# Local-and-global attention with an ELU feed-forward: scales of w_in from sums on ACT, three groups of weight pairs, zero matmuls between attention's steps

## The chip, the cores and the metric

The kernel runs on one core of one Trainium2 chip. The metric is the device time in microseconds of the execution, as the median of several runs. PE is the matrix engine (TensorE; PEld its weight loads), DVE the vector engine, ACT the scalar engine, POOL GpSimd, and SP the engine whose queue issues the transfers.

## The reference

Eight batches of eight heads with 512 local and 32 global positions of 64 elements. A local query sees the 32 global keys and the local keys at most 32 positions away; a global query sees everything. The 4608 rows of the result (512 wide) go through a feed-forward network.

```python
k_all = np.concatenate([k_g, k_l], axis=2);  v_all = np.concatenate([v_g, v_l], axis=2)
out_g = np.matmul(sm(scale * np.matmul(q_g, k_all.transpose(0, 1, 3, 2))), v_all)
s_ll = np.where(np.abs(pos[:, None] - pos[None, :]) <= 32, scale * (q_l @ k_l^T), -1e9)
a_l = sm(np.concatenate([scale * (q_l @ k_g^T), s_ll], axis=-1))
out_l = np.matmul(a_l, v_all)
x = concatenate([out_g, out_l], axis=2) as rows of 512
h = x @ w_in                                        # 512 x 2048
g = np.where(h > 0.0, h, np.exp(np.minimum(h, 0.0)) - 1.0)
return g @ w_out                                    # 2048 x 512
```

(The lines are shortened; `sm` is the softmax over the last axis.)

## The kernel before

**Attention** is a generator over slots. Each batch has ten: two for the global queries and eight local ones (two groups of four heads, four tiles of 128 queries). A slot has four steps, between which control is handed back: S (scores, `stage_s`, matmuls at L458; for a global slot `stage_ga`, L406), T and U (transposes of the probabilities, L494, two slots later) and V (values, `stage_v`, L516, three slots later). The index `i` of the main loop counts these steps. DVE adds the mask to the scores and takes the maximum (L469), ACT makes the exponentials (L476), POOL divides (L483).

**The feed-forward network** runs in fp16 with three products for each one (high x high, low x high, high x low). Its x is cut in 17 blocks of 256 rows, sixteen local ones and one with all the global rows; `split_x` makes the high and low parts of a block when attention has completed it. The 2048 inner columns are eight pairs of 2 x 128. For a block and a pair, `ffn1` makes the first half (24 matmuls, L231) and the elementwise step (ACT L239 and L240, POOL L241, DVE L246, ACT L248, DVE L249), and `ffn2`, two pairs later, the second half (12 matmuls, L273). Each half is cut in quanta, eight to a pair.

**The weights** arrive as 64-bit numbers and are converted on the chip, in 16 units: `unit(0, p)` for w_in, `unit(1, p)` for w_out. A unit is one load of 1 MB into one of two `raw` buffers, and then the steps `s0` to `s4`: ACT and POOL take the size of the value and clamp it (L151, L152), DVE puts the fp32 bits together in three passes (L156, L159, L163), the scale comes from a maximum (DVE, L168) for w_in and from a sum (ACT, L170) for w_out, ACT writes the high part (L181) and DVE the low one (L184). For w_in the scale is shared by all partitions: `all_max` transposes the column with a matmul (L106) and takes the maximum of it (L107).

**Groups.** A block's eight pairs can be done as one group ("f"), or, as long as not all weights are converted, in groups a, b, c, d of 1, 1, 2 and 4 pairs; `tables(group)` makes the factors of a group once its weights are there. Each group but the last of a block writes its partial output to `od` in DRAM; the next one reads it back and adds it on DVE (L281). `choose` takes the lowest ready block with a group that has its tables. Four blocks go through the groups; 13 go as "f".

**The order.** The main loop hands out steps of attention and quanta of the network by `PACE`, pairs of (step, quanta done by then), with straight lines between. Until the second entry's step `lead[0]` holds: attention runs alone. Units are started at listed steps, and later by a credit: 2 for each step of attention from 8 steps before the end of the lead, 1 for each quantum, and a unit for every `CONV` of it. `defer(n, fn)` runs a step n ticks later. The framework's scheduler then orders the instructions of each engine by their place in the program and by when it believes their inputs to be there, and inserts the semaphores. PSUM has two `h` buffers (values of attention in the lead, later the first halves), two `acc`, and four `pa`. Ten matmuls of zeros (`warm`, L117) stand at the start.

Of the kernel before, what the change touches and what calls it, by code (L numbers as in the profile page):

```python
# [10 lines left out]
F32 = mybir.dt.float32  # L11
F32R = mybir.dt.float32r
I32 = mybir.dt.int32
AF = mybir.ActivationFunctionType
ALU = mybir.AluOpType
# [6 lines left out]
DM, DF = 512, 2048  # L22
# [10 lines left out]
AHEAD = 2  # L33


PACE = ((0, 0), (66, 0), (112, 180), (320, 850))
WARM = 10
CONV = 14
NBL = B * SL // BLK
GROUPS = {"a": (0, 1), "b": (1, 2), "c": (2, 4), "d": (4, 8), "f": (0, 8)}  # L40
NX = 5


# [6 lines left out]
def attn_ffn(ctx: ExitStack, tc: tile.TileContext, qT, qgT, kT, vT, w_in, w_out, mask, out):  # L50
# [62 lines left out]
    wout = [wts.tile([P, NFT, DM], F16, name=f"wout{k}") for k in "hl"]  # L113
    warm = wout[0][:, NFT - 1, :]
    nc.vector.memset(warm, 0.0)
    for _ in range(WARM):
        nc.tensor.matmul(ps_o.tile([P, DM], F32, name="acc"), warm[:, 0:P], warm, start=True, stop=True)  # L117
    pww = wts.tile([P, NP], F32, name="pww")
    pwo = wts.tile([P, NP], F32, name="pwo")
    isc = wts.tile([P, NP], F32, name="isc")  # L120
# [13 lines left out]
    def unit(m, p):  # L134
        f = slice(2 * p * P, 2 * (p + 1) * P)
        shape = [P, NC, 2 * P] if m == 0 else [P, 2, DM]
        raw = ffn.tile([*shape, 2], I32, name="raw")
        if m == 0:
            nc.sync.dma_start(raw, w1[:, :, f, :])
            parts = [w[:, :, f] for w in win]  # L140
        else:
            nc.sync.dma_start(raw, w2[:, 2 * p:2 * p + 2, :, :])
            parts = [w[:, 2 * p:2 * p + 2, :] for w in wout]
        pw = (pww if m == 0 else pwo)[:, p:p + 1]
        u = ffn.tile(shape, F32, name="cu", bufs=3)
        mx = ffn.tile([P, 4], F32, name="cm", bufs=4)
        high, low = raw[..., 1], raw[..., 0]
        ui = u.bitcast(I32)

        def s0():  # L150
            nc.scalar.activation(u, high.bitcast(F32), AF.Abs)  # L151
            nc.gpsimd.tensor_scalar(u, u, FMAX, FMIN, ALU.min, ALU.max)  # L152

        def s1a():
            tc.keep_in_program_order(
                nc.vector.tensor_scalar(ui, ui, 3, 0x3ffffff8, ALU.logical_shift_left, ALU.bitwise_and))  # L156

        def s1b():
            nc.vector.scalar_tensor_tensor(out=ui, in0=high, scalar=-0x40000000, in1=ui,  # L159
                                           op0=ALU.bitwise_and, op1=ALU.bitwise_or)  # L160

        def s1c():
            nc.vector.scalar_tensor_tensor(out=ui, in0=low, scalar=29, in1=ui,  # L163
                                           op0=ALU.logical_shift_right, op1=ALU.bitwise_or)

        def s1d():
            if m == 0:
                nc.vector.tensor_reduce(out=mx[:, 0:1], in_=u, op=ALU.max, axis=AX.XY, apply_absolute_value=True)  # L168
            else:
                nc.scalar.activation(low.bitcast(F32), u, AF.Abs, accum_out=mx[:, 1:2])  # L170

        def s2():
            if m == 0:
                all_max(mx[:, 1:2], mx[:, 0:1])

        def s3():
            nc.vector.tensor_scalar_max(mx[:, 1:2], mx[:, 1:2], LOW)
            power(pw, mx[:, 1:2])
            nc.vector.reciprocal(mx[:, 2:3], pw)
            nc.vector.tensor_scalar_mul(mx[:, 3:4], mx[:, 2:3], 2.0 ** 14)  # L180
            nc.scalar.activation(parts[0], u, AF.Copy, scale=mx[:, 3:4])  # L181

        def s4():
            nc.vector.scalar_tensor_tensor(out=parts[1].rearrange("p a b -> p (a b)") if m else parts[1],  # L184
                                           in0=u.rearrange("p a b -> p (a b)") if m else u, scalar=mx[:, 3:4],
                                           in1=parts[0].rearrange("p a b -> p (a b)") if m else parts[0],
                                           op0=ALU.mult, op1=ALU.subtract)

        d = 1 if lead[0] else 2
        lag = 7 if m else 12  # L190
        for i, fn in ((1, s0), (1 + d, s1a), (1 + 2 * d, s1b), (1 + 3 * d, s1c), (1 + 4 * d, s1d),
                      (1 + lag, s2), (2 + lag, s3), (3 + lag, s4)):
            defer(i, fn)

    def tables(group):

        r = slice(*GROUPS[group])
        wm = wts.tile([P, 4], F32, name=f"wm_{group}")
        t = wts.tile([P, NP], F32, name=f"t_{group}")
        kk = wts.tile([P, NP], F32, name=f"kk_{group}")  # L200
        nc.vector.tensor_mul(t[:, r], pww[:, r], pwo[:, r])
        nc.vector.tensor_reduce(out=wm[:, 0:1], in_=t[:, r], op=ALU.max, axis=AX.X)

        def rest():
            all_max(wm[:, 1:2], wm[:, 0:1])
            nc.vector.reciprocal(wm[:, 2:3], wm[:, 1:2])
            nc.vector.tensor_scalar(t[:, r], pwo[:, r], wm[:, 2:3], 16.0, ALU.mult, ALU.mult)
            nc.vector.tensor_mul(kk[:, r], t[:, r], pww[:, r])
            nc.vector.tensor_scalar_mul(kk[:, r], kk[:, r], 2.0 ** -28)
            nc.vector.tensor_scalar_mul(isc[:, r], pww[:, r], -2.0 ** -28)  # L210
            tab[group] = wm[:, 1:2], t, kk

        defer(5, rest)
# [4 lines left out]
    def ffn_stream():  # L218
# [36 lines left out]
        def ffn2():  # L255
            job, p, gh, gl = pend.pop(0)
            group, blk, _, _, sc = job
            first, last = GROUPS[group][0], GROUPS[group][1] - 1
            if p == first:
                if group == "a":  # L260
                    od[blk] = dram.tile([2, P, DM], F32, name=f"od{blk}")
                state["acc"] = [ps_o.tile([P, DM], F32, name="acc") for _ in range(2)]
                state["o"] = [ffn.tile([P, DM], F32, name="o", bufs=3) for _ in range(2)]
                if group in "bcd":
                    for t in range(2):
                        nc.sync.dma_start(state["o"][t], od[blk][t])
            acc = state["acc"]
            for t in range(2):
                for j in range(2):
                    s = slice(j * BLK + t * P, j * BLK + (t + 1) * P)  # L270
                    f = 2 * p + j
                    for k, (gt, wt) in enumerate(((gh, wout[0]), (gh, wout[1]), (gl, wout[0]))):
                        nc.tensor.matmul(acc[t], gt[:, s], wt[:, f, :], start=p == first and j == 0 and k == 0,  # L273
                                         stop=p == last and j == 1 and k == 2)
                    if j == 0:
                        yield
                if p == last:
                    o = state["o"][t]
                    oc = sc[:, 2 * NP:2 * NP + 1]
                    if group in "bcd":  # L280
                        nc.vector.scalar_tensor_tensor(out=o, in0=acc[t], scalar=oc, in1=o,  # L281
                                                       op0=ALU.mult, op1=ALU.add)
                    else:
                        nc.scalar.activation(o, acc[t], AF.Copy, scale=oc)  # L284
                    nc.sync.dma_start(od[blk][t] if group in "abc" else out_rows(blk, t), o)
                yield

        def split_x(blk):
# [27 lines left out]
        def scales(group, mx):  # L316
# [3 lines left out]
            r = slice(*o)  # L320
            nc.gpsimd.tensor_scalar(sc[:, r], isc[:, r], mx[:, 2:3], 1.0, ALU.mult, ALU.mult)
            nc.gpsimd.tensor_scalar(sc[:, NP + o[0]:NP + o[1]], t[:, r], mx[:, 3:4], 1.0, ALU.mult, ALU.mult)
            nc.gpsimd.tensor_scalar(sc[:, 2 * NP:2 * NP + 1], wm, mx[:, 2:3], 2.0 ** -18, ALU.mult, ALU.mult)
            return sc

        order = list(range(NBL + 1))
# [8 lines left out]
        def choose():  # L335

            for blk in order:
                if blk in xs and xs[blk][3] and step[blk] < 4:
                    group = "f" if "f" in tab and not step[blk] else "abcd"[step[blk]]
                    if group in tab:  # L340
                        step[blk] += 4 if group == "f" else 1
                        xh, xl, mx, _ = xs[blk]
                        return group, blk, xh, xl, scales(group, mx)

# [5 lines left out]
        while left <= NBL:  # L350
# [8 lines left out]
            for p in range(lo, hi):  # L359
# [3 lines left out]
                    yield from ffn2()  # L363
                if p == hi - 1:
                    job = choose()
            if group in "df":
                del xs[blk]
                left += 1
        while pend:
# [8 lines left out]
    def attention():  # L378
# [189 lines left out]
        for i in range(n + LAGV):  # L568
# [3 lines left out]
            s1 = slots[i - LAGT] if LAGT <= i < n + LAGT else None  # L572
            s2 = slots[i - LAGV] if i >= LAGV else None
            for what in "STUV":
                if what in "TU" and s1 and s1[0] == "l":
                    if what == "T":
                        stage_tg(sts[s1[1]], s1[2], s1[3])
# [8 lines left out]


    f = ffn_stream()
    units = (u for g in "abcd" for u in load_weights(g))
    done = credit = 0  # L590

    def pace(i):
# [10 lines left out]
            next(units, None)  # L603

    for i, _ in enumerate(attention()):
        lead[0] = i < PACE[1][0]
        if i in (5, 12):
            next(units)
        elif i >= PACE[1][0] - 8:
            convert(2)  # L610
        want = pace(i)
        if lead[0]:
# [70 lines left out]
```

## Time and profile before

| | us |
|---|---|
| median of 3 runs | 1034.95 |
| lowest and highest run | 1033.44, 1039.45 |
| the profiled execution | 1034.22 |
| its span, first to last instruction | 1032.1 |
| PE, DVE, ACT, POOL busy | 987.5, 565.1, 526.6, 306.7 |

The mean granted clock of TensorE in it is 0.982 of full speed. Rows of the profile name the line of the program, the engine, the operation, output<-input by the program's names, the count (x) and durations; after a bar stands the time that the engine sat idle just before such an instruction, and what ended that. A matmul's duration includes its way through the array, so durations of consecutive matmuls overlap; the same holds, by some hundredths of a microsecond, on DVE.

### The profile page before, as it was taken

The page shows a single profiled execution, that of the slowest core. Times are in us where ns is not written, and L with a number is a line of the kernel's source. Part 1 is how long each engine was busy: PE and PEld are TensorE (multiplying, and loading weights), DVE is VectorE, ACT ScalarE, POOL GpSimd, SP SyncE. Part 2 cuts the span into 40 slices and gives each one's busy share as a digit, 9 for nine tenths or more (in the row PEclk, how much of TensorE's full clock was granted, in tenths as well). Part 3 has the DMA queues.
Part 4 walks back from the last instruction along what each step waited for, and adds up shares of the span by engine and source line. Part 5 has one row for each costly group of instructions (what it writes and reads, how often), then busy time and mean ns, then how long its engine had stood idle before and what let it go on. Part 6 is the DMA issues. An engine that isn't in the chain of part 4 may idle for free.

```text
span 1032.1 us, 18890 instructions
## 1 busy us (share of the span) xinstructions
PE 987.5 (96%) x7192; PEld 682.5 (66%) x7192; DVE 565.1 (55%) x1659; ACT 526.6 (51%) x1257; POOL 306.7 (30%) x549
## 2 busy tenths in 40 slices
PE   6899779899999999999999999999999999999996
PEld 4576555566676777766767667667677667666663
DVE  5789698894455555454555445454545454422221
ACT  4778675575344545455544544554545544434342
POOL 3456545344122232223222322232322222211110
PEclk9699899999999999999999999999999999999998
DMA  7546565451321122112310123012200100000000
GB/s 268 160 137 224 180 199 189 159 187 65 108 68 57 43 67 102 32 37 67 98 36 16 42 77 102 27 32 77 97 22 11 42 23 31 1 21 21 1 21 21
DMA packets 39154, 81.78 MB, mean 79 GB/s; under 512 B 3864, under 2 KB 5912, under 8 KB 39064
## 3 DMA queue, kind: packets, MB, share of 16 engines
q1 hardware_dynamic: 39064, 80.58, 23.6%
q8 instruction: 57, 0.93, 0.4%
q14 instruction: 33, 0.27, 0.1%
HBM read 65.36 MB, written 15.20 MB: 78 GB/s over the span
## 4 chain that ended last, share of the span: by engine, by line
PE 84%; DVE 6%; DMA 3%; POOL 2%; ACT 2%; issue 1%; SPq 0%; POOLq 0%; ACTq 0%
PE h L231 32%; PE acc L273 31%; PE pa L516 6%; PE pa L458 5%; PE pa L494 5%; PE pa L406 2%; DVE cu L159 1%; POOL p L483 1%; DMA k<-kT 1%; DVE cu L163 1%; PE acc L458 1%; PE h L516 1%; PE pa L440 1%; ACT p L476 1%; DMA raw<-w_out 1%
## 5 line engine op out<-in xcount | busy, mean ns | idle before, releaser
L231 PE MATMUL h<-xh,winh 128*128 128x256 f16 x1088 | 298.5, 275 | 11.2 <-DVE g L246 5.6
L231 PE MATMUL h<-xh,winl 128*128 128x256 f16 x1088 | 298.1, 274 | 0.0
L231 PE MATMUL h<-xl,winh 128*128 128x256 f16 x1088 | 298.0, 274 | 0.0
L231 PEld LDWEIGHTS <-winh 128*128 128x128 f16 x2176 | 209.8, 98 | 71.0 <-issue 18.7
L241 POOL TENSOR_SCALAR g<-g,xs 128x512 f32<-128x512 f32 x136 | 98.3, 723 | 389.8 <-ACT g L240 356.3
L273 PE MATMUL acc<-wouth,gh 128*128 128x512 f16 x544 | 207.4, 381 | 3.9 <-ACT o L284 2.4
L273 PE MATMUL acc<-woutl,gh 128*128 128x512 f16 x544 | 206.6, 380 | 0.0
L273 PE MATMUL acc<-wouth,gl 128*128 128x512 f16 x544 | 206.3, 380 | 0.0
L483 POOL TENSOR_SCALAR p<-p,sm 128x224 f32<-128x224 f32 x256 | 133.2, 537 | 194.7 <-DVE sm L481 77.8
L246 DVE SCALAR_TENSOR_TENSOR g<-h,kk_f,g 128x512 f32<-128x512 f32 x104 | 78.1, 751 | 195.6 <-POOL g L241 195.2
L248 ACT CAST gh<-g 128x512 f16<-128x512 f32 x136 | 83.8, 617 | 189.3 <-DVE g L246 188.9
L476 ACT ACTIVATE p<-p,m 128x224 f32<-128x224 f32 x256 | 120.1, 470 | 92.0 <-DVE m L472 91.3
L273 PEld LDWEIGHTS <-gh 128*128 128x128 f16 x1088 | 103.4, 98 | 95.8 <-issue 14.3
L239 ACT ACTIVATE g<-h,xs 128x512 f32<-128x512 f32 x136 | 92.7, 682 | 130.0 <-PE h L231 129.8
L249 DVE TENSOR_TENSOR gl<-g,gh 128x512 f16<-128x512 f32 x136 | 95.0, 699 | 46.2 <-ACT gh L248 45.0
L231 PEld LDWEIGHTS <-winl 128*128 128x128 f16 x1088 | 106.9, 98 | 13.9 <-issue 0.6
L273 PEld LDWEIGHTS <-gl 128*128 128x128 f16 x544 | 53.4, 98 | 63.9 <-issue 0.8
L469 DVE CUSTOM_DVE_ANT_0 p<-pa,msk 128x224 f32<-128x224 f32 x228 | 77.3, 384 | 20.1 <-PE pa L458 19.9
L497 DVE COPY pt<-pa 128x512 f32<-128x512 f32 x99 | 67.5, 682 | 36.6 <-PE pa L494 36.2
L240 ACT ACTIVATE g<-g 128x512 f32<-128x512 f32 x136 | 85.2, 628 | 3.4
L494 PE MATMUL pa<-ident,p 128*128 128x128 f32 x512 | 79.5, 278 | 6.8 <-POOL p L483 4.0
L494 PEld LDWEIGHTS pa<-ident,p 128*128 128x128 f32 x512 | 60.4, 142 | 19.8 <-POOL p L483 8.1
(159 smaller groups left out, 1001.7 us busy)
## 6 DMA issues: line engine op xcount, KB each, us to landing
v<-vT SPq DMA_DIRECT2D x64, 256.0 KB, 2.7
k<-kT SPq DMA_DIRECT2D x32, 448.0 KB, 3.6
out<-o SPq DMA_DIRECT2D x34, 256.0 KB, 2.0
q<-qT SPq DMA_DIRECT2D x32, 256.0 KB, 4.8
raw<-w_in SPq DMA_DIRECT2D x8, 1024.0 KB, 6.6
raw<-w_out SPq DMA_DIRECT2D x8, 1024.0 KB, 5.1
od<-o SPq DMA_DIRECT2D x24, 256.0 KB, 2.9
o<-od SPq DMA_DIRECT2D x24, 256.0 KB, 3.1
```

Of the source, the lines that this page charges most:

```text
L231: nc.tensor.matmul(h[:, j, :], wt[:, c, f], xt[:, c, :], start=k == 0, stop=k == 11)
L239: nc.scalar.activation(g, hf, AF.Relu, scale=sc[:, p:p + 1])
L240: nc.scalar.activation(g, g, AF.Exp, scale=-1.0)
L241: nc.gpsimd.tensor_scalar(g, g, -1.0, sc[:, NP + p:NP + p + 1], ALU.add, ALU.mult)
L246: nc.vector.scalar_tensor_tensor(out=g, in0=hf, scalar=kk[:, p:p + 1], in1=g, op0=ALU.mult, op1=ALU.max)
L248: nc.scalar.copy(gh, g)
L249: defer(1, lambda: nc.vector.tensor_sub(gl, g, gh))
L273: nc.tensor.matmul(acc[t], gt[:, s], wt[:, f, :], start=p == first and j == 0 and k == 0, stop=p == last and j == 1 and k == 2)
L469: nc.vector.tensor_tensor_reduce(out=p[:, 0:KW], in0=sp[r][:, j * KW:(j + 1) * KW], in1=msk[:, mi, :], op0=ALU.add, op1=ALU.max, scale=1.0 ...
L476: nc.scalar.activation(ps[i][:, 0:KW], ps[i][:, 0:KW], AF.Exp, bias=m[:, 1, i:i + 1], scale=scale, accum_out=s[:, 0, i:i + 1])
L483: nc.gpsimd.tensor_scalar(ps[i][:, 0:KW], ps[i][:, 0:KW], s[:, 1, i:i + 1], 1.0, ALU.mult, ALU.mult)
L494: nc.tensor.transpose(tp[:, (2 * r + i) * P:(2 * r + i + 1) * P], ps[2 * j + r][:, i * P:(i + 1) * P], ident)
```

## The change

- The scale of a w_in unit comes from the sum of sizes in each partition, made by ACT as for w_out, and no longer from DVE's maximum. The maximum over the partitions stays. Two powers of two make up for the larger scales.
- Three groups of 2, 2 and 4 pairs, a, b and c, take the place of four.
- The pace: attention runs alone for 58 steps, not 66, then more slowly mixed with the network up to step 92, and faster up to 116. Two more units start in the lead, at steps 21 and 29, so that the whole first group is converted there; the credit starts 4 steps ahead of the lead's end, and a unit costs 13 of it.
- `keep_warm` puts a matmul of zeros ahead of each S and each U step in the lead, 29 more than before, all into one `h` buffer that they hold.

```diff
-PACE = ((0, 0), (66, 0), (112, 180), (320, 850))
+PACE = ((0, 0), (58, 0), (92, 90), (116, 230), (320, 850))
-CONV = 14
+CONV = 13
-GROUPS = {"a": (0, 1), "b": (1, 2), "c": (2, 4), "d": (4, 8), "f": (0, 8)}
+GROUPS = {"a": (0, 2), "b": (2, 4), "c": (4, 8), "f": (0, 8)}
...
-    for _ in range(WARM):
-        nc.tensor.matmul(ps_o.tile([P, DM], F32, name="acc"), warm[:, 0:P], warm, start=True, stop=True)
+    def keep_warm(n):
+        if "h" not in spare:
+            spare["h"] = ps_h.tile([P, 2, BLK], F32, name="h").rearrange("p a b -> p (a b)")
+        for _ in range(n):
+            tc.keep_in_program_order(nc.tensor.matmul(spare["h"], warm[:, 0:P], warm, start=True, stop=True))
+    spare = {}
+    keep_warm(WARM)
...
         def s1d():
-            if m == 0:
-                nc.vector.tensor_reduce(out=mx[:, 0:1], in_=u, op=ALU.max, axis=AX.XY, apply_absolute_value=True)
-            else:
-                nc.scalar.activation(low.bitcast(F32), u, AF.Abs, accum_out=mx[:, 1:2])
+            nc.scalar.activation(low.bitcast(F32), u, AF.Abs, accum_out=mx[:, m:m + 1])
...
-            nc.vector.tensor_scalar(t[:, r], pwo[:, r], wm[:, 2:3], 16.0, ALU.mult, ALU.mult)
+            nc.vector.tensor_scalar(t[:, r], pwo[:, r], wm[:, 2:3], 64.0, ALU.mult, ALU.mult)
...
             for what in "STUV":
+                if lead[0] and what in "SU":
+                    keep_warm(1)
...
-        lead[0] = i < PACE[1][0]
-        if i in (5, 12):
+        lead[0] = i + 1 < PACE[1][0]
+        if i in (5, 13, 21, 29):
             next(units)
-        elif i >= PACE[1][0] - 8:
+        elif i >= PACE[1][0] - 4:
             convert(2)
```

The scheduler decides what this does to each engine's order. Line numbers of the changed kernel are 5 higher from the middle on. PE, near the start of attention, before (`pa<-k,qg` are scores of global queries, `k,q` of local ones, `ident,pg` and `ident,p_81` transposes of probabilities):

```order
L406 MATMUL pa<-k,qg 128x272 x4
L458 MATMUL acc<-k,q 128x224 x4
L458 MATMUL pa<-k,q 128x224 x4
L406 MATMUL pa<-k,qg 128x272 x2
L440 MATMUL pa<-ident,pg 128x128
```

and now:

```order
L411 MATMUL pa<-k,qg 128x272 x4
L122 LDWEIGHTS wouth
L122 MATMUL h<-wouth 128x512
L122 LDWEIGHTS wouth
L122 MATMUL h<-wouth 128x512
L463 MATMUL acc<-k,q 128x224 x4
L122 LDWEIGHTS wouth
L122 MATMUL h<-wouth 128x512
L122 LDWEIGHTS wouth
L122 MATMUL h<-wouth 128x512
L463 MATMUL pa<-k,q 128x224 x4
```

The zero matmuls (`h<-wouth`) stand between the steps of attention; further on one or two stand ahead of each group of transposes or scores.

DVE, at the end of the conversion, before (`woutl` is the low part of the last unit, `kk_d` and `kk_f` the factors of the last group and of "f", `g<-h,kk_d` the elementwise step of a pair):

```order
L206 RECIPROCAL wm_d<-wm_d 128x1
L207 TENSOR_SCALAR t_d<-pwo,wm_d 128x4
L208 TENSOR_TENSOR kk_d<-t_d,pww 128x4
L209 TENSOR_SCALAR kk_d<-kk_d 128x4
L107 TENSOR_REDUCE wm_f<-pa 128x1
L206 RECIPROCAL wm_f<-wm_f 128x1
L207 TENSOR_SCALAR t_f<-pwo,wm_f 128x8
L208 TENSOR_TENSOR kk_f<-t_f,pww 128x8
L209 TENSOR_SCALAR kk_f<-kk_f 128x8
```

and now:

```order
L213 TENSOR_TENSOR kk_c<-t_c,pww 128x4
L213 TENSOR_TENSOR kk_f<-t_f,pww 128x8
L214 TENSOR_SCALAR kk_c<-kk_c 128x4
L214 TENSOR_SCALAR kk_f<-kk_f 128x8
L251 SCALAR_TENSOR_TENSOR g<-h,kk_a,g 128x512
L502 COPY pt<-pa 128x4x128 x2
L254 TENSOR_TENSOR gl<-g,gh 128x512
L251 SCALAR_TENSOR_TENSOR g<-h,kk_a,g 128x512
L254 TENSOR_TENSOR gl<-g,gh 128x512
L251 SCALAR_TENSOR_TENSOR g<-h,kk_c,g 128x512
```

The last tables stand behind 12 elementwise steps of pairs now, behind 16 before; the next two steps are of the fourth block's first group, and then the last group begins.

SP, the loads, before (`raw` is a unit's load):

```order
L139 DMA raw<-w_in 128x4x512
L398 DMA v<-vT 128x512
L142 DMA raw<-w_out 128x2x1024
L383 DMA k<-kT 128x896 x2
L388 DMA q<-qT 128x512 x2
L398 DMA v<-vT 128x512 x2
L383 DMA k<-kT 128x896 x2
L398 DMA v<-vT 128x512
L388 DMA q<-qT 128x512 x2
```

and now:

```order
L147 DMA raw<-w_in 128x4x512
L403 DMA v<-vT 128x512
L150 DMA raw<-w_out 128x2x1024
L388 DMA k<-kT 128x896 x2
L393 DMA q<-qT 128x512
L403 DMA v<-vT 128x512
L393 DMA q<-qT 128x512
L147 DMA raw<-w_in 128x4x512
L403 DMA v<-vT 128x512
L388 DMA k<-kT 128x896 x2
L393 DMA q<-qT 128x512 x2
L403 DMA v<-vT 128x512
```

The first two loads here are those of units 3 and 4 in both; the load of unit 5 now stands ahead of the k, q and v of later slots, where there was none.

More of the change, by code (lines that the diff above doesn't have):

```diff
@@ L263, in ffn2 @@
                 state["o"] = [ffn.tile([P, DM], F32, name="o", bufs=3) for _ in range(2)]
-                if group in "bcd":
+                if group in "bc":
                     for t in range(2):
@@ L279, in ffn2 @@
                     oc = sc[:, 2 * NP:2 * NP + 1]
-                    if group in "bcd":
+                    if group in "bc":
                         nc.vector.scalar_tensor_tensor(out=o, in0=acc[t], scalar=oc, in1=o,
@@ L284, in ffn2 @@
                         nc.scalar.activation(o, acc[t], AF.Copy, scale=oc)
-                    nc.sync.dma_start(od[blk][t] if group in "abc" else out_rows(blk, t), o)
+                    nc.sync.dma_start(od[blk][t] if group in "ab" else out_rows(blk, t), o)
                 yield
@@ L322, in scales @@
             nc.gpsimd.tensor_scalar(sc[:, NP + o[0]:NP + o[1]], t[:, r], mx[:, 3:4], 1.0, ALU.mult, ALU.mult)
-            nc.gpsimd.tensor_scalar(sc[:, 2 * NP:2 * NP + 1], wm, mx[:, 2:3], 2.0 ** -18, ALU.mult, ALU.mult)
+            nc.gpsimd.tensor_scalar(sc[:, 2 * NP:2 * NP + 1], wm, mx[:, 2:3], 2.0 ** -20, ALU.mult, ALU.mult)
             return sc
@@ L337, in choose @@
             for blk in order:
-                if blk in xs and xs[blk][3] and step[blk] < 4:
-                    group = "f" if "f" in tab and not step[blk] else "abcd"[step[blk]]
+                if blk in xs and xs[blk][3] and step[blk] < 3:
+                    group = "f" if "f" in tab and not step[blk] else "abc"[step[blk]]
                     if group in tab:
-                        step[blk] += 4 if group == "f" else 1
+                        step[blk] += 3 if group == "f" else 1
                         xh, xl, mx, _ = xs[blk]
@@ L365, in ffn_stream @@
                     job = choose()
-            if group in "df":
+            if group in "cf":
                 del xs[blk]
@@ L588, in attn_ffn @@
     f = ffn_stream()
-    units = (u for g in "abcd" for u in load_weights(g))
+    units = (u for g in "abc" for u in load_weights(g))
     done = credit = 0
```

## The prediction

> **What bounds the kernel now.** I read the page first, for the shares and the clock, then stages, then the chain of waits, then the groups of one stage.
>
> ```profile
> span 1032.1 us, 18890 instructions
> PE 987.5 (96%) x7192; PEld 682.5 (66%) x7192; DVE 565.1 (55%) x1659; ACT 526.6 (51%) x1257; POOL 306.7 (30%) x549
> PEclk9699899999999999999999999999999999999998
> ```
>
> TensorE looks full everywhere, and the clock row dips only in the first slices. The stages below (stretch, its length, then busy time of PE, PEld, DVE, ACT, POOL, then granted clock) tell more.
>
> ```profile
> 0.00:20.00 20.00, 15.49 (x78) 9.67 (x78) 8.39 (x51) 10.19 (x32) 6.46 (x21) 0.91 0.87 319
> 20.00:77.50 57.50, 49.67 (x338) 34.60 (x337) 45.88 (x200) 39.12 (x127) 27.21 (x52) 0.85 0.44 143
> 77.50:238.00 160.50, 137.56 (x963) 93.72 (x962) 140.12 (x359) 108.74 (x229) 82.44 (x120) 0.97 0.57 189
> 238.00:1022.00 784.00, 783.96 (x5816) 544.38 (x5816) 370.69 (x1051) 367.65 (x869) 190.62 (x358) 1.00 0.14 46
> 1022.00:1032.10 10.10, 0.78 (x4) 0.17 (x2) 0.00 (x0) 0.95 (x2) 0.00 (x0) 0.67 0.17 52
> ```
>
> From 238 us on TensorE never stops, at full clock: that stage is the sum of its matmuls. The loss lies before. How much real work stands there is read from the chain, where a piece's length is the distance to the next one and not the pipelined duration:
>
> ```profile
> 69.69 0.87 PE pa L494 x8
> 71.81 0.96 PE pa L458 x8
> 72.77 1.14 PE h L516 x16
> 238.04 2.78 PE h L231 x24
> 240.82 2.59 PE acc L273 x12
> 243.41 2.62 PE h L231 x24
> ```
>
> So a pair of the FFN costs 2.62 + 2.59 = 5.21 us of TensorE, and an attention slot 0.96 (scores) + 0.87 (transposes) + 1.14 (values), near 3 us. Counted in the order of the instructions, 18 first halves, 16 second halves, 23 score slots, 20 of transposes and 19 of values stand ahead of the matmul at 238.04: 47.2 + 41.4 + 22.1 + 17.4 + 21.7, with small ones under 170 us. Nearly 70 us are lost there.
>
> In 77.5 to 238 DVE is busy 140.1 of 160.5 us, ACT 108.7, POOL 82.4. Instructions of DVE overlap by some 0.07 us at their ends, so this is close to all it can do. DVE converts the weights there, and 238.04 is where the last weights' tables are ready and the last group's pairs follow. DVE sets when that is:
>
> ```profile
> L159 DVE SCALAR_TENSOR_TENSOR cu<-raw,cu 128x1024 int32<-128x1024 int32 x16 | 22.3, 1399 | 0.1
> L163 DVE SCALAR_TENSOR_TENSOR cu<-raw,cu 128x1024 int32<-128x1024 int32 x16 | 20.9, 1308 | 0.1
> L168 DVE TENSOR_REDUCE cm<-cu 128x1 f32<-128x1024 f32 x8 | 9.6, 1201 | 0.0
> L281 DVE SCALAR_TENSOR_TENSOR o<-acc,xs,o 128x512 f32<-128x512 f32 x16 | 11.7, 739 | 0.3 <-PE acc L273 0.3
> L249 DVE TENSOR_TENSOR gl<-g,gh 128x512 f16<-128x512 f32 x16 | 11.3, 709 | 3.3 <-ACT gh L248 3.3
> L246 DVE SCALAR_TENSOR_TENSOR g<-h,kk_a,g 128x512 f32<-128x512 f32 x4 | 3.0, 744 | 2.2 <-POOL g L241 2.2
> L246 DVE SCALAR_TENSOR_TENSOR g<-h,kk_b,g 128x512 f32<-128x512 f32 x4 | 2.9, 747 | 5.9 <-POOL g L241 5.9
> L469 DVE CUSTOM_DVE_ANT_0 p<-pa,msk 128x224 f32<-128x224 f32 x56 | 19.1, 381 | 1.3 <-PE pa L458 1.0
> L480 DVE TENSOR_SCALAR sm<-sm 128x4 f32<-128x4 f32 x20 | 3.7, 185 | 0.6 <-ACT p L476 0.3
> L497 DVE COPY pt<-pa 128x512 f32<-128x512 f32 x10 | 6.8, 684 | 4.3 <-PE pa L494 4.2
> ```
>
> **The change part by part.** I compare the same event in both kernels: the pair whose first matmul must wait for the elementwise step that stands behind the last tables on DVE. Before it is pair 19 (at 238.04). In the changed order it is pair 15, since only 12 elementwise steps, not 16, stand ahead of those tables. Before that event the changed order has 14 first halves, 12 second halves, 19 score slots, 18 of transposes, 16 of values.
>
> Work that DVE no longer does ahead of it, each duration less the 0.07 of overlap:
> - The maxima of w_in: 8 x 1.13 = 9.0 us.
> - Additions to the partial output (L281 before): 16 become 6, 10 x 0.67 = 6.7 us.
> - Elementwise steps of pairs, 4 fewer: 4 x (0.68 + 0.64) = 5.3 us.
> - Four score slots fewer. A score addition goes every 0.32 us, its accumulator's read included:
>
> ```profile
> 212.63 0.38 DVE L469 CUSTOM_DVE_ANT_0 p<-pa,msk 128x224 f32<-128x224 f32 x1
> 212.95 0.38 DVE L469 CUSTOM_DVE_ANT_0 p<-pa,msk 128x224 f32<-128x224 f32 x1
> ```
>
>   4 x (4 x 0.32 + three small ones of 0.12) = 6.6 us. Two copies of transposes fewer, 1.2 us, and a few maxima of x, about 0.7.
>
> Together 29.5 us of DVE, so the event comes that much sooner if DVE idles as before.
>
> TensorE's work that then still lies ahead: 4 x 2.62 + 4 x 2.59 + 4 x 0.96 + 2 x 0.87 + 3 x 1.14 = 29.9 us, call it 30, which is paid at the end, one for one. So the regrouping and the pace by themselves come to -29.5 + 30 = +0.5: later FFN work eats what the earlier release gives. The gain must come from idle time of DVE.
>
> Idle time of DVE in 77.5 to 238 is 160.5 - 140.1 = 20.4 us. Most of what is named stands at the elementwise steps (5.9, 2.2 and 3.3 in the rows above). With 4 of 18 such steps fewer I take 4/18 of it, -4.5 us. Bounds: 0, if the waits only move, and -20.4.
>
> Idle time in 20 to 77.5 is 57.5 - 45.9 = 11.6 us. The first four units, not two, are converted there now, and one score slot less stands ahead of the first pair, so the same DVE work meets less attention. From 47 to 77 us TensorE is full while DVE has gaps; a unit's passes need no matmul and fit them. I take about half, -5.5. Bounds: 0 and -11.6.
>
> The sums move to ACT:
>
> ```profile
> L170 ACT ACTIVATE raw<-cu 128x1024 f32<-128x1024 f32 x8 | 9.1, 1139 | 4.0 <-DVE cu L163 4.0
> L170 ACT ACTIVATION_READ_ACCUMULATOR raw<-cu 128x1 f32 x8 | 1.4, 179 | 0.0
> ```
>
> 8 x (1.14 + 0.18) = 10.5 us more on ACT, which has 160.5 - 108.7 = 52 us free in that stage: 0 on the path. If that cover is gone the cost is at most those 10.5. Its 4.0 us of waiting for DVE can double, and exponentials of attention queue behind a sum; both lie in that room. The sum writes into the raw tile, so a w_in tile's buffer comes free one step later.
>
> The zero matmuls: 39 instead of 10, 29 x 2.59/12 = 6.3 us of TensorE. Each is ahead of the first FFN pair, where 70 us are lost, so I cost them at 0. Where TensorE is full, from 47 us, about half of them stand, 3 us; the slot that no longer stands ahead of the first pair, 3 us, covers those. Without that cover: +3, at worst +6.3.
>
> The transfers: 24 writes and 24 reads of partial outputs become 16 and 16.
>
> ```profile
> od<-o SPq DMA_DIRECT2D x24, 256.0 KB, 2.9
> o<-od SPq DMA_DIRECT2D x24, 256.0 KB, 3.1
> 25.14 0.38 SPq L139 DMA_DIRECT2D raw<-w_in  x1
> 35.14 0.38 SPq L142 DMA_DIRECT2D raw<-w_out  x1
> 44.86 5.53 SPq L398 DMA_DIRECT2D v<-vT  x2
> ```
>
> They land in 3 us under other work: 0. The raw loads of units 3 and 4 were already issued at 25 and 35 us. Now units 5 and 6 follow in SP's queue ahead of k, q and v, and wait for a raw buffer there; who waits behind is attention's next slot. The nearest row is the 5.5 us that the loads of v waited; SP works two slots ahead, so 0, with +5.5 as the end. Fewer scale triples on POOL: 0, POOL is half idle.
>
> Sum: 1034.2 (the profiled execution, 1032.1 of span and 2.1 around it, 0.7 under the median of 1034.95) - 29.5 + 30 - 4.5 - 5.5 = 1024.7, call it **1025**.
>
> **The clock.** In 20 to 77.5 the granted clock is 0.85, and TensorE then waits for others, as here before scores:
>
> ```profile
> 25.45 1.86 PE L458 MATMUL acc<-k,q 64*128 64x224 f32 x4 [3.75 <-DVE m L469]
> ```
>
> If the zero matmuls held full clock there, its 49.7 us of work would shrink by 0.15 x 49.7 = 7.5 us. By my sum this is idle time of TensorE under DVE, worth nothing; as a rival below it is on the path. [...]
>
> **The rivals.**
> - Nothing of the idle time is saved: +0.5 alone gives 1034.7, with 2 or 3 us of waits saved 1032: within the bound. For it: DVE's queue is in order, and a wait avoided at one step shows up at the next. Against it: fewer steps have those waits.
> - The clock is on the path: 1025 - 7.5 = 1017.5. For it: TensorE is full for the last 30 us of this stage. Against it: the slow part lies before, where DVE and POOL end the waits.
> - Slower: the zero matmuls hold one of the two h buffers as long as attention runs alone, so the values of a slot wait until ACT's copy and DVE's addition have emptied the other.
>
> ```profile
> DVE xglob L527 <- ACT xr L520: 13.1, 11, 2.1
> ```
>
>   DVE comes to that addition behind unit passes of up to 1.4 us. Eight slots go that way; at 2.1 us each (the longest wait in the row) it is 17 us, 1042. It decides from 10 us, 1.25 per slot, on. Against it: values are issued a slot, some 4 us, apart.
>
> **How the numbers follow.** My forecast (idle time saved) 0.40; the clock on the path 0.12; nothing saved 0.32; the h buffer 0.16. Half a per cent, 5.2 us, is about what a measurement of this kernel can tell from no change. Faster is the first two, 0.52; same 0.32; slower 0.16. The range runs from 1015 (the clock and a bit of the 20.4 us) to 1038 (nothing saved and the zero matmuls' 3 us on the path), leaving the worst of the h buffer outside.
>
> **What would show it.** Right: TensorE full from about 200 us on, not 238; DVE over 88% busy between the first pair and that point; no reductions of w_in on DVE; the clock near full before 60 us. Wrong: the first FFN pair later than 80 us with values waiting for DVE; gaps of TensorE after 200 us; SP waiting for a raw buffer with scores waiting for k or q; the release at 205 us or later, which would leave no gain.

## The result and the profile after

| | before | after |
|---|---|---|
| median of 20 runs, us | 1033.64 | 1040.28 |
| lowest and highest, us | 1031.09, 1042.40 | 1037.90, 1045.37 |
| the profiled execution, and its span, us | 1034.22, 1032.1 | 1045.37, 1043.6 |

The ratio of the times is 1.0052, with a 95% interval from 1.0032 to 1.0072: half a per cent slower, where 1025 us were forecast. The profiled execution of after is the longest of its 20 and has a mean clock of 0.972, where the 20 have 0.979: the two traces differ by 11.5 us, the medians by 6.6. So the trace shows the loss in the right places, but larger than it usually is.

The page of after, its shares and the clock row:

```profile
span 1043.6 us, 18875 instructions
PE 999.7 (96%) x7220; PEld 688.5 (66%) x7220; DVE 551.8 (53%) x1639; ACT 538.0 (52%) x1269; POOL 296.4 (28%) x537
PEclk9679989989999999999999999999999999999998
```

DVE has 13 us less to do and ACT 11 us more, as the change says. The stages of after, cut at the first FFN matmul (86.5 us) and at pair 15's first half, the release (columns as before):

```profile
0.00:20.00 20.00, 17.70 (x90) 9.61 (x90) 9.25 (x53) 9.76 (x32) 7.32 (x21) 1.00 0.88 320
20.00:86.50 66.50, 57.27 (x311) 38.05 (x311) 47.23 (x188) 41.60 (x120) 27.85 (x48) 0.74 0.46 147
86.50:218.30 131.80, 108.77 (x760) 74.65 (x759) 106.76 (x294) 98.39 (x207) 58.85 (x92) 0.94 0.47 156
218.30:1032.00 813.70, 813.70 (x6053) 565.36 (x6054) 388.59 (x1106) 386.90 (x912) 202.34 (x379) 1.00 0.16 50
```

Three readings. From the release on TensorE works without a gap, for 816.0 us to the end of its last matmul at 1034.3 us, where it was 784.7 us to 1022.8: 31 us of work moved behind the release. The release came at 218.3 and not at 238.0, 19.8 us sooner; 31.2 less 19.8 is 11.4, nearly all of the 11.5 us that the trace is longer. And the lead lasts until 86.5 us at a clock of 0.74, where it ended at 77.5 at 0.85: DVE is idle for 66.5 - 47.2 = 19.3 us of it, and for 131.8 - 106.8 = 25.0 us of the next stage, 44.3 together against 32.0 before.

The change without the zero matmuls between the steps (`no_zero`, below; 1.0000), cut inside its first pair's first half, from where that runs on, and at 207.3 us, from where TensorE is full:

```profile
20.00:75.30 55.30, 45.09 (x305) 31.78 (x305) 47.10 (x190) 42.00 (x119) 29.36 (x50) 0.88 0.55 177
75.30:207.30 132.00, 108.19 (x760) 74.42 (x759) 108.73 (x297) 97.34 (x206) 62.22 (x89) 0.94 0.48 156
207.30:1022.00 814.70, 814.70 (x6048) 565.38 (x6047) 386.96 (x1104) 385.02 (x911) 202.51 (x378) 1.00 0.15 49
```

The two later stages are as long as in after, and the lead is 11.2 us shorter. The first cut isn't the same event in both: five matmuls of the first half go at 70.1 to 71.2 us in no_zero, the others from 74.8 on, and in after the first comes at 86.5. An event that can be compared is the first scores behind 18 matmuls of that half:

```profile
76.28 1.03 PE L463 MATMUL pa<-k,q 64*128 64x224 f32 x8
```

in no_zero, and in after:

```profile
88.61 1.03 PE L463 MATMUL pa<-k,q 64*128 64x224 f32 x8
```

From there to 207.3 and 218.3 us it is 131.0 and 129.7 us. So what the zero matmuls do to these traces, they do ahead of the first pair.

### The profile page after: what moved, and what is told of

Its sections match the earlier page's. It is cut to its first block, busy times and chain, and to the rows that moved or that the text cites. A ratio compares the mean times of both kernels' runs of the same rounds, so it can differ in the third digit from the quotient of the medians.

```text
span 1043.6 us, 18875 instructions
## 1 busy us (share of the span) xinstructions
PE 999.7 (96%) x7220; PEld 688.5 (66%) x7220; DVE 551.8 (53%) x1639; ACT 538.0 (52%) x1269; POOL 296.4 (28%) x537
## 4 chain that ended last, share of the span: by engine, by line
PE 85%; ACT 5%; DVE 4%; DMA 2%; POOL 2%; issue 1%; POOLq 0%; ACTq 0%
PE h L236 32%; PE acc L278 32%; PE pa L521 5%; PE pa L463 5%; PE pa L499 5%; PE pa L411 2%; ACT p L481 1%; DMA raw<-w_out 1%; DMA raw<-w_in 1%; PE h L521 1%; ACT raw L175 1%; PE h L122 1%; DVE cu L171 1%; ACT cu L159 1%; PE acc L463 1%
## 5 line engine op out<-in xcount | busy, mean ns | idle before, releaser
L488 POOL TENSOR_SCALAR p<-p,sm 128x224 f32<-128x224 f32 x256 | 128.1, 516 | 218.2 <-DVE sm L486 135.9
L502 DVE COPY pt<-pa 128x512 f32<-128x512 f32 x103 | 70.0, 681 | 28.7 <-PE pa L499 28.3
L499 PEld LDWEIGHTS pa<-ident,p 128*128 128x128 f32 x512 | 62.5, 145 | 16.2 <-POOL p L488 4.7
```

The lines of the kernel that those rows point to most:

```text
L488: nc.gpsimd.tensor_scalar(ps[i][:, 0:KW], ps[i][:, 0:KW], s[:, 1, i:i + 1], 1.0, ALU.mult, ALU.mult)
L499: nc.tensor.transpose(tp[:, (2 * r + i) * P:(2 * r + i + 1) * P], ps[2 * j + r][:, i * P:(i + 1) * P], ident)
```

## The experiments

All are timed against the kernel before on the same chip; the mean clock is that of all timed runs of the kernel.

| run | sums on ACT | groups and pace | zero matmuls in the lead | ratio (95%) | clock |
|---|---|---|---|---|---|
| after | yes | new | 29, holding an h buffer | 1.0052 (1.0032 to 1.0072) | 0.979 |
| no_zero | yes | new | none | 1.0000 (0.9974 to 1.0026) | 0.978 |
| no_sum | no | new | holding | 1.0060 (1.0031 to 1.0088) | 0.977 |
| old_groups | yes | old | holding | 1.0044 (1.0017 to 1.0070) | 0.984 |
| sum_only | yes | old | none | 1.0041 (1.0015 to 1.0067) | 0.977 |
| groups_only | no | new | none | 1.0031 (1.0008 to 1.0055) | 0.976 |
| zero_only | no | old | holding | 1.0029 (1.0000 to 1.0059) | 0.979 |
| small_zero | yes | new | holding, 64 columns | 1.0105 (1.0074 to 1.0136) | 0.970 |
| hold_h | yes | new | one, holding | 1.0061 (1.0033 to 1.0089) | 0.971 |
| empty_act | yes | new | holding, emptied by ACT | 1.0035 (1.0008 to 1.0063) | 0.978 |
| zero_inplace | yes | new | 24 in place | 1.0005 (0.9980 to 1.0030) | 0.982 |
| hold_inplace | yes | new | in place, and one holding | 1.0034 (1.0015 to 1.0054) | 0.979 |
| elsewhere | yes, other tile | new | none | 1.0023 (1.0004 to 1.0043) | 0.979 |
| elsewhere_old | yes, other tile | old | none | 1.0001 (0.9974 to 1.0028) | 0.981 |
| old_inplace | no | old | 28 in place | 1.0016 (0.9983 to 1.0049) | 0.986 |
| old_inplace3 | no | old | 84 in place | 1.0095 (1.0062 to 1.0127) | 0.985 |
| old_inplace_else | yes, other tile | old | in place | 1.0004 (0.9976 to 1.0033) | 0.986 |

A letter of a theory in the expectations holds for the runs that were planned together; in others the same letter can stand for another theory. The ten zero matmuls at the start write into `acc` in before, zero_inplace and the three old_inplace runs, and into an h buffer in all others, as in after.

### One part at a time

`no_zero` takes out the zero matmuls between the steps, `no_sum` the sums, `old_groups` the groups, pace, units and credit; `sum_only`, `groups_only` and `zero_only` leave one part alone.

```diff
 no_zero:
-                if lead[0] and what in "SU":
-                    keep_warm(1)
 no_sum:
-            nc.scalar.activation(low.bitcast(F32), u, AF.Abs, accum_out=mx[:, m:m + 1])
+            if m == 0:
+                nc.vector.tensor_reduce(out=mx[:, 0:1], in_=u, op=ALU.max, axis=AX.XY, apply_absolute_value=True)
 ...
 ...
 old_groups, here against after:
+PACE = ((0, 0), (66, 0), (112, 180), (320, 850))
+CONV = 14
+GROUPS = {"a": (0, 1), "b": (1, 2), "c": (2, 4), "d": (4, 8), "f": (0, 8)}
 ...
```

> The changed kernel without the zero matmuls between attention's steps (the ten at the start stay). Theory Z, the zero matmuls take TensorE's time while it sets the pace of the lead: the first pair comes 6 to 9 us sooner than at 86.6 us, and the whole is 6 to 9 us faster than the changed kernel, 1031 to 1034, ratio to before 0.997 to 1.000. Theory W, ACT and SP stand still in the lead for the raw loads of units 5 and 6, whose buffers the sums hold: the first pair stays at 84 us or later, the gap of ACT ahead of the step that sizes unit 6 stays, ratio 1.003 to 1.007. Theory C, the zero matmuls keep the clock up: slower than the changed kernel, ratio above 1.007, clock in the lead below 0.74.

> The changed kernel with the scales of w_in taken from DVE's maxima again, with the two powers of two that belong to them. Theory Z: 8 times 1.2 us come back to DVE, which ends the conversion, and the whole is 4 to 9 us slower than the changed kernel, ratio to before 1.009 to 1.014. Theory W (the sum on ACT holds raw one step longer and blocks ACT, so that conversion waits for loads): the raw loads of w_out come sooner, and the whole is the same or faster than the changed kernel, ratio 0.998 to 1.005.

> The changed kernel with the groups, the pace, the two units in the lead and the credit of before; the sums on ACT and the zero matmuls stay. Theory Z: the zero matmuls are 33 here (8 steps more), so the lead is 4 to 8 us longer than before, minus what the sums free on DVE, up to 9: ratio 0.996 to 1.004. Theory W: two units in the lead cause no late load there, the release comes at 229 to 235 us with 18 pairs done, and the whole is 4 to 9 us faster than before, ratio 0.991 to 0.996.

> The kernel before with only the sums of w_in on ACT (and their powers of two). Both theories: 8 times 1.13 us leave DVE, which is busy 140 of 160 us ahead of the release, so 4 to 9 us faster than before, ratio 0.991 to 0.996. If ACT's later release of raw costs as much as DVE gains, 0.998 to 1.002, and the release stays at 238 us.

> The kernel before with the groups, the pace, the units in the lead and the credit of the changed one; maxima on DVE, no zero matmuls between the steps. Theory R (a sum that writes into raw keeps the load buffer until ACT has come to it, and the chain sum, load, sizes on ACT, sets the end of the conversion): the release comes sooner than the 207 us that the same kernel has with the sums, although DVE has 9 us more to do; 3 to 6 us faster than before, ratio 0.994 to 0.997. Rival D (DVE's work alone sets it): 9 us of maxima come back and the release moves to about 216 us; 6 to 9 us slower than with the sums, ratio 1.005 to 1.009.

> The kernel before with only the zero matmuls between the steps (33 in its longer lead) and the h buffer that they hold. With only two units in the lead DVE comes to its additions soon: theory H gives 0 to 3 us of loss, ratio 0.999 to 1.003. Rival: the buffer costs as much whatever DVE does, ratio 1.004 to 1.007.

Measured: the zero matmuls cost 0.3% with the maxima (groups_only to no_sum, before to zero_only; each is hardly more than its uncertainty), 0.5% with both other parts, and nothing that shows on top of the sums with the old groups. Without them the change is worth nothing. The parts don't add up: sums and groups cost 0.4% and 0.3% alone and nothing together. Each edit also makes the scheduler write another order; whether that is the reason isn't shown.

Of the expectations, theory Z holds for no_zero in its time, though the first pair came 16 us sooner and not 6 to 9. no_sum is nearer to W than to Z, and zero_only lies in H. old_groups is at the upper edge of Z. sum_only and groups_only missed both of their ranges: the sums alone did not bring 4 to 9 us but cost 4, and the groups alone fell between the two theories.

### What of the zero matmuls costs

`small_zero` leaves an eighth of their TensorE time and the same held buffer; `hold_h` leaves the hold and a single zero matmul, ahead of the scores of slot 14, the last of the lead; `empty_act` lets ACT alone empty the other buffer, so that DVE's addition reads from SBUF; `zero_inplace` writes the zeros into the tile that the scores or transposes behind them overwrite.

```diff
 small_zero:
+            tc.keep_in_program_order(nc.tensor.matmul(spare["h"][:, 0:w], warm[:, 0:P], warm[:, 0:w], start=True, stop=True))
 ...
-                    keep_warm(1)
+                    keep_warm(1, 64)
 hold_h:
-                if lead[0] and what in "SU":
+                if (i, what) == (14, "S"):
                     keep_warm(1)
 empty_act:
 ...
+            part = pv[:, :, P:GW]
+            if lead[0]:
+                part = xpart
+                nc.scalar.copy(part, pv[:, :, P:GW])
 ...
-                    nc.vector.tensor_add(xg, xg, pv[:, :, P:GW])
+                    nc.vector.tensor_add(xg, xg, part)
 zero_inplace:
             halves = [ps_a.tile([P, 512], F32, name="pa") for _ in range(2)]
+            zero(halves[0])
 ...
+            if j:
+                zero(tp)
 ...
```

> The changed kernel with the 29 zero matmuls between the steps 64 columns wide and not 512: same places, an eighth of their time on TensorE. Theory T (their time on TensorE is the cost, 29 times 0.22 at full and 0.43 us at half clock): as fast as without them, ratio to before 0.998 to 1.002. Rival H (the h buffer that they hold, or the order that they force): as slow as the changed kernel, ratio 1.004 to 1.007.

> The changed kernel with one zero matmul at the end of the lead in the place of the 29: it holds the h buffer just as long, and costs 0.2 us of TensorE. Theory T: as fast as without them, ratio to before 0.998 to 1.002. Rival H (the buffer): as slow as the changed kernel, ratio 1.004 to 1.007, with the first pair at 84 us or later, not 76.

> The changed kernel, zero matmuls and held buffer as they are, but in the lead ACT copies the global part of a slot's values out of the h buffer too (about 0.2 us each) and DVE adds it from SBUF. Theory H with DVE as the one that empties late: values follow each other sooner, the first pair comes 4 us or more before 86.6 us, ratio to before 0.999 to 1.003. If ACT's copy, which stands before it, is what comes late: no change, 1.004 to 1.007.

> The changed kernel with the zero matmuls written into the tile that the next scores or transposes overwrite, so that they hold no h buffer; 27 of them, as many columns as before. Theory H (the held h buffer is the cost): the first pair comes at 80 us or sooner, and the whole is as fast as without zero matmuls, ratio to before 0.997 to 1.002; under 0.997 only if the clock in the lead rises above 0.89 as well. Rival T (their time, or the order that they force): ratio 1.004 to 1.007.

Measured: the hold alone, with one matmul, costs as much as all 29 (1.0061). Written in place, 24 of them (not the 27 of the expectation) cost nothing that shows (1.0005), so the hold is what costs. `empty_act` loses a third less than after (1.0035); it lies between its two ranges, and that difference is smaller than the uncertainty. `small_zero`, with an eighth of TensorE's time, is the worst of all and above both of its ranges: that time can't be the main cost. The traces divide the runs in the same way. The first FFN matmul starts at 70.1 us in no_zero and at 71.3 in zero_inplace; with the hold it starts at 79.6 in hold_h (H had 84 or later), 80.2 in empty_act, 85.9 in small_zero and 86.5 in after. But the clock of small_zero, 0.970, is also the lowest, and that led to the last group of runs.

The values of the lead in the trace of after, TensorE's timeline (start, modelled duration, tile, count; the last ones with `h` as output):

```profile
53.38 2.19 PE L521 MATMUL h<-pt,v 128*64 128x160 f32 x16
58.87 1.21 PE L521 MATMUL h<-pt,v 128*64 128x160 f32 x16
65.87 1.21 PE L521 MATMUL h<-pt,v 128*64 128x160 f32 x16
73.31 2.19 PE L521 MATMUL h<-pt,v 128*64 128x160 f32 x16
78.40 1.21 PE L521 MATMUL h<-pt,v 128*64 128x160 f32 x16
```

and of no_zero:

```profile
58.25 1.21 PE L521 MATMUL h<-pt,v 128*64 128x160 f32 x16
...
65.32 1.21 PE L521 MATMUL h<-pt,v 128*64 128x160 f32 x16
```

One set of values goes every 5 to 7 us, and the last starts at 78.4; with both buffers free it starts at 65.3. ACT's copy of the values (L525) is what waits for them, 17.0 us in 6 waits in after, against 0.7 in no_zero and 5.4 in hold_h:

```profile
  ACT xr L525: 17.0, 6
```

```profile
  ACT xr L525: 0.7, 2
```

```profile
  ACT xr L525: 5.4, 3
```

### By waits or by the clock

Within one kernel the executions with the lower mean clock are the longer ones. Of 125 runs of the kernel before, the 34 at a clock up to 0.978 have a median of 1041.6 us, the 41 from 0.979 to 0.982 have 1034.2, the 50 above have 1032.5; the correlation is -0.95. So the question was whether the hold costs by making the values wait, or by lowering the clock: hold_h stands at 0.971, no_zero at 0.978. `hold_inplace` adds the hold to zero_inplace; the others put zero matmuls in place into the kernel before.

```diff
 hold_inplace, on zero_inplace (its ten at the start write into h again):
 ...
             for what in "STUV":
+                if (i, what) == (14, "S"):
+                    keep_warm(1)
 old_inplace3, on old_inplace:
         if lead[0]:
-            for _ in range(1):
+            for _ in range(3):
                 tc.keep_in_program_order(nc.tensor.matmul(tile, warm[:, 0:P], warm, start=True, stop=True))
 old_inplace_else, on old_inplace:
+            nc.scalar.activation(parts[0], u, AF.Abs, accum_out=mx[:, m:m + 1])
 ...
```

> The changed kernel without the zero matmuls that hold the h buffer, with a single one that holds it to the end of the lead (as in hold_h) and with zero matmuls written in place into the tiles of scores and transposes (as in the kernel that has only those, 1.0005). Theory H (the values' own waits cost the time): the waits are the same as in hold_h, ratio 1.005 to 1.007 whatever the clock. Theory C (the waits cost by lowering the clock, about 7 us for 0.01 of the mean): the mean clock of the runs comes back from 0.971 to 0.978 or more, and the ratio to 1.000 to 1.002. Either is refuted if clock and time move against each other.

> The kernel before (its groups, pace and maxima) with zero matmuls written in place between the lead's steps, 28 of them, no buffer held. Theory C: the third of the runs of before that stand at a clock under 0.978 and 1038 to 1044 us goes or becomes rare, the mean clock rises from 0.981 to 0.984 or more and the mean time falls by 2 us, ratio 0.998. Theory T (their TensorE time, 28 x 0.22 = 6 us, half of it where TensorE is full): ratio 1.002 to 1.003. Theory N (the clock in the lead is worth nothing): 1.000 with any clock.

> As old_inplace with three zero matmuls at each place. Theory C: the clock of the lead close to 1 from 20 us on, mean clock 0.986 or more, ratio 0.997 less what their 18 us of TensorE cost. Theory T: three times the cost of old_inplace, ratio 1.006 or more. A ratio above that of old_inplace at a higher clock says that the clock is bought too dear.

> The groups and pace of before, the sums of w_in on ACT with their elementwise output in a tile that no load waits for, and the zero matmuls in place: the three parts that cost nothing or bring something, together. Theory C: as old_inplace, 0.997 to 0.998, since the sums by themselves stood at 1.0001. Theory N: 1.000.

Measured: neither theory alone. With the gaps filled the hold costs 0.3% (1.0005 to 1.0034), not the 0.6% of hold_h over no_zero, and the clock is 0.979, not 0.971. Each of the halves is about as large as the uncertainty of one ratio, so the split is rough. A wait that is left stands in TensorE's timeline of hold_inplace:

```profile
25.11 1.22 PE L531 MATMUL h<-pt,v 128*64 128x160 f32 x6 [4.91 <-DVE xglob L540]
```

TensorE sat idle for 4.9 us until DVE had copied the global part out of the other `h` buffer; in zero_inplace TensorE has no idle time just ahead of values up to 90 us. The traces also show the clock's side. From 40 to 50 and from 50 to 60 us it is 0.54 and 1.00 in no_zero, 0.83 and 1.00 in zero_inplace, 0.81 and 1.00 in hold_inplace, but 0.51 and 0.50 in hold_h and 0.50 and 0.65 in after. So in the traces with the held buffer, and without zeros in place, the half clock lasts longer. By estimate, ten more microseconds at 0.50 are up to 5 us of TensorE's work.

The clock can't be bought, though. `old_inplace` has the clock at 0.91 and 1.00 in 20 to 40 and 40 to 60 us, where before had 0.63 and 0.94:

```profile
20.00:40.00 20.00, 13.34 (x85) 8.43 (x81) 18.92 (x66) 13.19 (x34) 8.81 (x13) 0.91 0.59 187
40.00:60.00 20.00, 19.70 (x169) 14.23 (x170) 14.92 (x73) 15.18 (x54) 9.89 (x23) 1.00 0.52 174
```

and before:

```profile
20.00:40.00 20.00, 13.38 (x61) 8.92 (x60) 16.55 (x56) 10.36 (x26) 6.67 (x9) 0.63 0.46 145
40.00:60.00 20.00, 19.55 (x140) 13.47 (x137) 14.10 (x66) 14.71 (x50) 11.57 (x23) 0.94 0.58 193
```

The kernel is no faster for it, 1.0016, and neither is old_inplace_else, 1.0004: theory C fell, and T and N of old_inplace can't be told apart. Three at each place (old_inplace3, where T holds) are 56 more zero matmuls of 0.216 us (2.59 / 12, by the row of twelve matmuls of the same 128x512 form), 12.1 us, at the same mean clock, and cost 0.0079 x 1033.5 = 8.2 us, with an uncertainty of some 5: about two thirds of a zero matmul's time, 0.15 us, is on the path there. With the new groups that price isn't seen: 24 x 0.15 would be 3.6 us, and zero_inplace stands 0.5 us over no_zero. So the 5.4 us that after loses over no_zero are shown for the zeros and the hold together, and hold_h shows that the hold alone is enough; a share for the zeros' own time isn't shown. Why small_zero is 0.4% slower than hold_h, at the same clock (0.970 and 0.971), stays open.

### Where the sum's output goes

The sum's elementwise output, which nobody reads, goes into the raw tile and holds it. `elsewhere` (new groups) and `elsewhere_old` put it into the place of the high part.

```diff
-            nc.scalar.activation(low.bitcast(F32), u, AF.Abs, accum_out=mx[:, m:m + 1])
+            nc.scalar.activation(parts[0], u, AF.Abs, accum_out=mx[:, m:m + 1])
```

> The changed kernel without the zero matmuls between the steps, and with the elementwise output of every sum written into the place of the high part, which is written over later, and not into raw. Nothing else differs: same sums on ACT, same durations. Theory R: raw comes free after DVE's last pass, 1 to 3 us sooner for each of ten later units; the release comes 5 to 15 us before 207 us, ratio to before 0.985 to 0.996. Rival Q (the in-order queue of ACT, in which the sums stand ahead of attention's exponentials, is the cost): no change, ratio 0.998 to 1.003.

> The kernel before with only the sums, whose elementwise output goes into the place of the high part and not into raw. The sums alone cost 1.0041. Theory R (with the groups of before, a sum that writes into raw delays the next load: 103.6 us for 97.2 us at the sixth unit): that cost goes, ratio 0.996 to 1.001. Rival Q (the place of the sum in ACT's queue, or the order that follows from it): still 1.002 to 1.006.

Measured with the old groups: 1.0041 becomes 1.0001. SP's queue in sum_only, two loads of w_out:

```profile
103.55 0.38 SPq L150 DMA_DIRECT2D raw<-w_out  x1
119.81 0.38 SPq L150 DMA_DIRECT2D raw<-w_out  x1
```

and in before:

```profile
97.23 0.38 SPq L142 DMA_DIRECT2D raw<-w_out  x1
113.76 0.38 SPq L142 DMA_DIRECT2D raw<-w_out  x1
```

The loads go 6 us later when a sum sits between the last pass and the next load; in elsewhere_old they go at 96.8 and 111.5, so the output in the raw tile is what made them late. That these loads are the whole 0.4% isn't shown: the mean clock of sum_only is lower too, 0.977 against 0.981. With the new groups the other tile brings nothing, as rival Q had it (1.0023 against 1.0000), so there the price of the raw tile isn't shown; why the two orders differ stays open.

## Why the prediction was wrong, point by point

On the scale of the forecast (1034.2 before, 1025 after) the measured ratio gives 1039.6, 15 us more. Two terms make up that distance: 10 us of DVE's idle time that were to be saved and were not, and 5.4 us for the zero matmuls, which stood at 0.

- **Work of DVE ahead of the release, -29.5.** Held. Without the zero matmuls TensorE is full from 207.3 us on, 30.7 us sooner than 238.04, and DVE's work from 20 us to there fell from 186.0 to 155.8 us. The chain of waits of no_zero has pair 15's first half there, with a gap inside (4.46 us where it takes 2.79):

```profile
205.61 4.46 PE h L236 x24
210.07 2.59 PE acc L278 x12
```

- **TensorE's work pushed behind it, +30.** Held: to the end of the last matmul it is 816.0 us, in after and in no_zero, against 784.7. These two terms cancel, and no_zero measures 1.0000.
- **Idle time of DVE, -4.5 and -5.5.** Failed, with or without the zeros. In no_zero the lead's idle time fell from 11.6 to 8.2 us, and that of the next stage rose from 20.4 to 132.0 - 108.7 = 23.3: together 31.5 against 32.0, where 22 were forecast. This is the larger of the two errors. Fewer steps with waits did not mean less waiting; what took the place of the waits saved was not traced one by one. The rival "nothing of the idle time is saved" describes no_zero; it was given 0.32.
- **Zero matmuls, 0.** Failed, and this step made the change slower and not equal. The 70 us that TensorE loses ahead of the release were taken as cover. They are no cover for a held buffer: with it and one zero matmul the time is 6.3 us over no_zero (hold_h), and 24 zero matmuls without it are 0.5 us over it (zero_inplace). The term measured +5.4 us. That lies inside the bound of 6.3 by luck, since the bound counted TensorE's time and not the buffer.
- **The rival of the held h buffer, 1042, at 0.16.** It came true in place and sign. That its 1042 is near to 1040.28 is luck: it put 17 us on a sum with 10 us of savings that did not come, and the zeros and the hold measured 5.4. The argument against it, values a slot apart, did not hold: the gap of 4.9 us in hold_inplace ended when DVE came to its copy. It was drawn as a wait alone; how much goes through the longer half clock isn't shown.
- **Sums on ACT, 0.** Right by the room on ACT, wrong by the raw tile that was named and not priced: with the old groups the sums cost 4 us, and nothing that shows with their output elsewhere. And the 9.0 us that DVE no longer works buy nothing by themselves: in elsewhere_old the release stands where it stood:

```profile
238.46 2.78 PE h L236 x24
```

  DVE's 8 us less work in that stage became idle time (76 to 238.5 us: 162.5 - 132.0 = 30.5 us idle, against 20.4):

```profile
76.00:238.50 162.50, 140.17 (x955) 95.76 (x953) 132.04 (x350) 116.45 (x244) 81.62 (x119) 0.94 0.56 184
```

  So "DVE sets when that is" was too strong: DVE was 87% busy there, but taking the maxima from it moved the release only with the new groups. There groups_only, with the maxima, has it at 211.6 us, and no_zero and elsewhere, without them, have it at 207.3 and 210.1: 1 to 4 us of the 9.
- **The clock, worth nothing on the path.** Not safe as a reason: runs of one kernel differ by 9 us along with it (1041.6 against 1032.5 us in the 125 above), whichever is the cause. Right as a result: raising it with zeros gains nothing (zero_inplace 1.0005, old_inplace 1.0016), so the rival of 1017.5 fell. That zero matmuls between the steps would hold full clock, which its 7.5 us and the mark of a clock near full before 60 us used, was the author's assumption, and no run shows it for after: its clock did not even rise, 0.74 in the lead against 0.85 before. Written in place they raised it, to 0.91 and 1.00 in 20 to 40 and 40 to 60 us of old_inplace, and saved no time.
- **What would show it.** Most of the marks named for "wrong" came: the first pair after 80 us (86.5) with values one by one, gaps of TensorE after 200 us, and the release after 205 us (218.3). SP did wait for raw buffers that a sum held, 40.6 us in all from 20 to 218 us, but no scores waited for k or q, and no_zero has as much of it (42.9). Of the marks for "right" only the missing reductions came; DVE was busy for 81% of the stage up to the release, not 88.

## What to carry to other kernels

A filler instruction is priced by what it holds as well as by its time: write it into a tile that the next real instruction overwrites anyway, and not into one of two buffers in rotation (0.5 us against 5.4 here). Idle time of an engine is cover only if the work is late there for another reason (the 70 us counted here did not cover the 6.3 us of hold_h); ask for each gap whether the filler would stand ahead of something that just became ready. When an engine is relieved of work, the time comes back only if nothing else, a load that waits for a tile or a chain through other engines, ends at the same moment (of the 9.0 us taken from DVE here the release moved by 1 to 4 with the new groups, and by none with the old). And fewer steps with waits are no forecast of less waiting (31.5 us of idle DVE against 32.0 here): price it at 0 until a trace shows which wait goes.

## What the hardware did that was not expected

The half clock did not go with busy time, where the prediction had named a clock near full before 60 us as a mark. In after TensorE has no idle time from 40 to 58 us, two microseconds to a row, and the clock stays at 0.50 for 16 us:

```profile
42.00:44.00 2.00, 2.00 (x11) 1.27 (x10) 1.48 (x4) 1.79 (x8) 1.92 (x4) 0.50 0.98 294
...
54.00:56.00 2.00, 2.00 (x15) 1.21 (x11) 2.00 (x9) 0.39 (x2) 1.80 (x2) 0.50 0.10 34
56.00:58.00 2.00, 2.00 (x15) 1.80 (x14) 1.95 (x13) 2.00 (x3) 1.80 (x4) 0.76 0.48 131
```

It went there, from 0.97 in 38 to 40 us, after a gap of 2.41 us ahead of scores at 39.9 us:

```profile
39.91 1.86 PE L463 MATMUL pa<-k,q 64*128 64x224 f32 x4 [2.41 <-ACT pt L451]
```

So here a gap of 2.41 us was followed by the half clock, and 16 us of busy rows passed before it ended; what sets it isn't shown. The matmuls there are small fp32 ones, and their ends are modelled, so short idle times between them could be hidden; whether that is the reason wasn't tried. The cause of the two clocks of before's runs (1041.6 us at up to 0.978, 1032.5 above 0.982) stays open as well: a late event may lower the clock, or the clock make the event late.
